# Shared gate and up matmuls at three unit boundaries of an interleaved convolution and FFN kernel

## The chip, the cores and the metric

The kernel runs on one core of one Trainium2 chip. The metric is the device time of one execution in microseconds; less is better. The matrix engine is called TensorE (PE in the profile, its weight loads PEld), the others VectorE (DVE), ScalarE (ACT), GpSimd (POOL) and SyncE (SP), which here only issues DMAs. Matmuls write to PSUM, and VectorE or ScalarE must copy ("evacuate") a result from there before its buffer is free again.

## The reference

Two layers of the same two blocks, on x of 2048 rows and 512 columns (D), in bf16. Block A is a gated long convolution over the rows, block B a SwiGLU feed-forward network with F = 1792:

```python
def _A_ref(q, k, v, shift_k, ssm_k, ssm_D):      # cut to what matters
    k_shift = sum(k_pad[:, t:t + S, :] * shift_k[:, ks - 1 - t] for t in range(4))
    kv = k_shift * v
    y = irfft(rfft(kv_pad) * rfft(kf_pad))[:S]    # causal convolution with ssm_k, by column
    return q * (y + kv * ssm_D)

def _B_ref(x, w_gate, w_up, w_down):
    return (silu(x @ w_gate) * (x @ w_up)) @ w_down

x = A_q
x = x + _A_ref(_layernorm(x), A_k, A_v, A_shift_k, A_ssm_k, A_ssm_D)
x = x + _B_ref(_layernorm(x), B_w_gate, B_w_up, B_w_down)
x = x + _A_ref(_layernorm(x), A_k, A_v, A_shift_k, A_ssm_k, A_ssm_D)
x = x + _B_ref(_layernorm(x), B_w_gate, B_w_up, B_w_down)
```

The convolution's result y depends on k, v and ssm_k alone, so both layers use the same y.

## The kernel before, in words

**Blocks and units.** The rows are cut into four blocks c of 512 rows. A partition p holds four rows (4p to 4p+3) of a block, so a tile of a block is 128 partitions x 4 x 512. A unit (layer, c, h) is one half of a block in one layer: h = 0 holds rows 0 and 2 of each partition, h = 1 rows 1 and 3, 256 rows in all (W). The units follow one another as (0, c, 0), (0, c, 1), (1, c, 0), (1, c, 1) for c = 0 to 3.

**Convolution.** `conv(c)` transforms block c of the kernel and of kv by matmuls with cosine and sine tables (`by_residue`, `direct`), combines spectra on VectorE (`butterfly4`, `product`) and transforms back (`inverse`) to y of that block. Block 0 is done first, in a form of its own (`half`, `direct`, `inverse_half`), since all else waits for it. Blocks 2 and 3 are worked in between the units.

**Prologue.** `prologue(layer, c, h)` normalises a unit's rows, multiplies by y, adds to x, normalises again to z and turns z around into zT, so that the columns of D lie on the partitions: 128 x 4 (contraction tiles) x 256 rows. SP's DMA transposes do the turning (line 893), but for the first unit, where TensorE does (line 920). The statistics of a normalisation are taken by VectorE (`ln_stats`, line 809) or, for chosen units, by ScalarE (`ln_stats_act`): there a Copy with an accumulated sum per row (line 828), a step that scales the sums to negative means (`nm`, line 831), a Square around the mean (line 834), a step that makes the variance (line 838); the power of -1/2 is taken on GpSimd.

**FFN.** `ffn(unit)` goes over the 14 column tiles of F in groups of 4, 4, 4 and 2 (`GROUPS`). For each pair of column tiles TensorE computes gate and up: the weight's 128 x 128 tile is the stationary operand, zT's 256 columns move, four matmuls are added up for a tile, and two tiles fill a PSUM buffer of 512 columns (ring `pf`, line 311 through `mm`). ScalarE evacuates the gate with Silu (line 970) and the up part with a copy (line 974), VectorE multiplies the two of a whole group (line 977), and the down matmuls (line 990, ht stationary, 512 columns of w_down moving) add into two accumulators `pd`, one for each row of the partition. At a unit's end ScalarE copies them (line 1034), VectorE adds them to x (line 1037), and in layer 1 SP stores the rows (line 1045). The last unit, (1, 3, 1), splits its last accumulator by columns, 256 and 256: VectorE finishes one half (line 1008), ScalarE the other (line 1011), and each is stored by its own queue (line 1014).

**What sets the order.** Every step is registered by `plan.add` in program order with its engine, the buffers that it reads and writes and an assumed cost. A table written out by hand, `ORDER`, has one number for each step, its place; `Plan.order` sorts by it, and each engine issues its steps in that order, SP's DMAs too. Buffers of a ring (four `pf`, two `pd`, five `ht`, two `sg`, three `zT`) are handed out along that order. `Plan.issue` emits the steps, and where the plan has a hole on TensorE ahead of 32 us it puts in matmuls of no use (`warm`, line 1267) on a tile of constants, `wz`:

```python
if start < warm_until and start - t > 0.5:
    ...
    n = int((start - max(t, 0.3) - 0.3) / 0.106)
    if n > 0:
        warm(ring, i, n)
```

Waits between engines are worked out from the buffers' regions when the program is built.

Of the kernel before, what the change touches and what calls it, by code (L numbers as in the profile page):

```python
# [18 lines left out]
NB = 4  # L19
# [31 lines left out]
LASTV = True  # L51
ORDER = [
# [58 lines left out]
]  # L111
R = 4

# [125 lines left out]
def kernel(  # L239
# [984 lines left out]
    def run(unit):  # L1224
        ffn(unit)
# [75 lines left out]
```

## Time and profile before

| | |
|---|---|
| median of 3 runs | 344.79 us (344.21 to 345.18) |
| the profiled execution | 344.93 us |
| its span, from the first to the last instruction | 343.2 us |
| TensorE busy | 336.4 us, 2579 matmuls |
| VectorE, ScalarE, GpSimd busy | 283.4, 253.9, 35.3 us |
| DMA | 22.95 MB, 67 GB/s in the mean |
| first gate matmul | 33.6 us |

The profile is of one execution. A row of a group has the line of the kernel, the engine, the operation, what it writes and reads, the shape, how many, the busy time and the mean of one. Matmuls are pipelined: the duration that a record gives is longer than the time from one start to the next, so the time that a stream of them takes is read from the chain of work in order of time, where each piece has its start, its length and its count. "<-" behind a time names what ended the idle time before it. A few matmul records are missing from the trace.

### The profile page before, as it was taken

What the parts mean: (1) busy time and instruction counts of PE and PEld (TensorE: products, weight loads), DVE (VectorE), ACT (ScalarE), POOL (GpSimd) and SP (SyncE); (2) the same over time, 40 slices, a digit from 0 to 9 for tenths busy, and PEclk for the clock granted to TensorE, in tenths of its full rate; (3) what the DMA queues carried; (4) which work ended last, traced back from release to release, by engine and by line L of the source; (5) the groups of instructions that cost most, each with busy time, mean ns of one, the idle gap of its engine ahead of it and who ended that gap; (6) DMA issues with size and microseconds to landing.
All of it is one profiled execution on the core that took longest, in us unless ns stands there. A gap on an engine that the chain in (4) does not pass through costs nothing.

```text
span 343.2 us, 6553 instructions
## 1 busy us (share of the span) xinstructions
PE 336.4 (98%) x2579; PEld 248.6 (72%) x2610; DVE 283.4 (83%) x482; ACT 253.9 (74%) x504; POOL 35.3 (10%) x46
## 2 busy tenths in 40 slices
PE   8999999999999999999999999999999999999996
PEld 7756868768687676858586777768685877777783
DVE  8899999899999999899999999989998433726022
ACT  6999999899997765958789995779475464446261
POOL 4010100203111000103110100201101001000000
PEclk9999999999999999999999999999999999999999
DMA  7999218310116044040101014210101100110101
GB/s 273 336 316 341 52 27 112 77 32 0 34 31 94 14 95 138 2 94 3 32 2 46 2 46 79 76 32 1 32 0 33 35 13 0 39 39 8 24 26 37
DMA packets 42088, 22.95 MB, mean 67 GB/s; under 512 B 33861, under 2 KB 39882, under 8 KB 42058
## 3 DMA queue, kind: packets, MB, share of 16 engines
q1 hardware_dynamic: 41904, 22.47, 26.6%
q8 instruction: 20, 0.33, 0.4%
q14 instruction: 10, 0.08, 0.1%
q10 hardware_dynamic: 154, 0.07, 0.1%
HBM read 12.33 MB, written 2.10 MB: 42 GB/s over the span
## 4 chain that ended last, share of the span: by engine, by line
PE 91%; ACT 4%; DVE 3%; issue 1%
PE pf L311 54%; PE pd L990 28%; PE ps L311 6%; PE ps L458 1%; ACT H L419 1%; PE wm L1267 1%; DVE bnst L809 1%; ACT hs L487 1%; PE pt L477 1%; ACT X L419 0%; ACT n L859 0%; PE pt L366 0%; DVE m L540 0%; DVE t L665 0%; DVE Z L667 0%
## 5 line engine op out<-in xcount | busy, mean ns | idle before, releaser
L311 PE MATMUL pf<-zT,wu_sb 128*128 128x256 bf16 x896 | 110.4, 273 | 0.1
L311 PE MATMUL pf<-zT,wg_sb 128*128 128x256 bf16 x896 | 110.2, 273 | 0.2
L990 PE MATMUL pd<-wd_sb,ht 128*128 128x512 bf16 (+1 forms) x440 | 102.4, 372 | 1.2
L311 PEld LDWEIGHTS <-wu_sb 128*128 128x128 bf16 x896 | 87.7, 98 | 16.4
L311 PEld LDWEIGHTS <-wg_sb 128*128 128x128 bf16 x896 | 87.6, 98 | 16.5 <-issue 0.8
L974 ACT CAST ht<-pf 128x512 bf16<-128x512 f32 x112 | 64.0, 591 | 29.3 <-PE pf L311 29.1
L970 ACT ACTIVATE sg<-pf 128x512 bf16<-128x512 f32 x112 | 65.5, 603 | 17.4 <-PE pf L311 15.1
L990 PEld LDWEIGHTS <-ht 128*128 128x128 bf16 x462 | 45.2, 98 | 42.5
L977 DVE TENSOR_TENSOR ht<-ht,sg 128x1024 bf16<-128x1024 bf16 (+1 forms) x64 | 39.0, 617 | 24.0 <-ACT sg L970 18.7
L814 POOL TENSOR_TENSOR rstd<-ve,nhalf 128x2 f32<-128x2 f32 x24 | 23.0, 958 | 217.8 <-DVE ve L812 207.6
L1034 ACT CAST dn<-pd 128x512 bf16<-128x512 f32 x30 | 17.0, 589 | 21.0 <-PE pd L990 20.9
L809 DVE BATCH_NORM_STATS2 bnst<-xc 128x6 f32<-128x512 bf16 x48 | 31.6, 684 | 0.6
L419 ACT ACTIVATE X<-ps 128x512 bf16<-128x512 f32 x32 | 19.2, 611 | 4.0 <-PE ps L311 3.4
L653 DVE TENSOR_TENSOR t<-X,G 128x2048 bf16<-128x2048 bf16 x18 | 21.9, 1218 | 0.1
L657 DVE TENSOR_TENSOR t<-X,G 128x2048 bf16<-128x2048 bf16 x18 | 21.9, 1216 | 0.0
L1037 DVE TENSOR_TENSOR xc<-xc,dn 128x1024 bf16<-128x1024 bf16 x15 | 10.3, 689 | 13.4 <-ACT dn L1034 13.2
L665 DVE TENSOR_TENSOR t<-t,t 128x2048 bf16<-128x2048 bf16 x12 | 14.7, 1222 | 0.3
L667 DVE TENSOR_TENSOR Z<-Z,t 128x2048 bf16<-128x2048 bf16 x12 | 14.6, 1220 | 0.2
L840 POOL TENSOR_TENSOR rstd<-ve,nhalf 128x2 f32<-128x2 f32 x8 | 8.7, 1088 | 59.2 <-ACT ve L838 59.1
L419 ACT ACTIVATE H<-ps 128x512 bf16<-128x512 f32 x24 | 13.8, 610 | 0.1
L886 DVE TENSOR_TENSOR n<-n,Yk 128x1024 bf16<-128x1024 bf16 x15 | 10.3, 688 | 4.1 <-ACT n L859 3.8
L604 ACT ACTIVATE kc<-kTb,tapF 128x512 bf16<-128x512 bf16 x16 | 12.1, 783 | 0.0
(105 smaller groups left out, 323.3 us busy)
## 6 DMA issues: line engine op xcount, KB each, us to landing
hn<-in_A_ssm_k_dram SPq DMA_DIRECT2D x4, 512.0 KB, 4.1
vt<-in_A_v_dram SPq DMA_DIRECT2D x4, 512.0 KB, 5.9
xc<-in_A_q_dram SPq DMA_DIRECT2D x4, 512.0 KB, 5.3
out_dram<-xc SPq DMA_DIRECT2D x15, 128.0 KB, 1.8
wg_sb<-in_B_w_gate_dram SPq DMA_DIRECT2D x1, 1792.0 KB
wu_sb<-in_B_w_up_dram SPq DMA_DIRECT2D x1, 1792.0 KB, 8.5
wd_sb<-in_B_w_down_dram SPq DMA_DIRECT2D x1, 1280.0 KB, 12.0
kn<-in_A_k_dram SPq DMA_DIRECT2D x1, 512.0 KB, 4.5
```

The costliest lines, as they stand in the source:

```text
L311: nc.tensor.matmul(o, lhsT=lhsT, rhs=rhs, start=(n == 0), stop=(n == len(terms) - 1))
L419: add("ACT", act(D), lambda: nc.scalar.activation(out=view(), in_=ps.t[:], func=ACT.Copy, scale=scale), r=[ps], w=[(buf, keys)], conv=conv)
L653: dve(n * D, lambda t1=t1, part=part: nc.vector.tensor_mul(out=t1.t[:], in0=x.t[:, sl, 0, :], in1=g.t[:, sl, part, :]), [(x, key(slots, (0 ...
L657: dve(n * D, lambda t2=t2, part=part: nc.vector.tensor_mul(out=t2.t[:], in0=x.t[:, sl, 1, :], in1=g.t[:, sl, 1 - part, :]), [(x, key(slots ...
L665: dve(n * D, lambda t1=t1, t2=t2, comb=comb: nc.vector.tensor_tensor(out=t1.t[:], in0=t1.t[:], in1=t2.t[:], op=comb), [t2], [t1], conv=conv)
L809: add("DVE", 0.6, lambda st=st, i=i: nc.vector.bn_stats(out=st.t[:], in_=xs[c].t[:, i, :]), r=[(xs[c], (i,))], w=[st])
L814: add("POOL", pw, lambda: nc.gpsimd.tensor_tensor(out=rstd.t[:], in0=ve.t[:], in1=nhalf.t[:].to_broadcast((P, n)), op=ALU.pow), r=[ve, nha ...
L970: add("ACT", act(D), lambda ps=ps, o=o, sg=sg: nc.scalar.activation(out=sg.t[:, o:o + 2, :], in_=ps.t[:], func=ACT.Silu), r=[ps], w=[(sg, ...
L974: add("ACT", act(D), lambda ps=ps, o=o, ht=ht: nc.scalar.copy(out=ht.t[:, o:o + 2, :], in_=ps.t[:]), r=[ps], w=[(ht, (o // 2,))], due=(uni ...
L977: dve(n * W, lambda sg=sg, ht=ht: nc.vector.tensor_mul(out=ht.t[:], in0=ht.t[:], in1=sg.t[:]), [sg], [ht], due=(unit, k / pairs, 0.0, "h"))
L990: nc.tensor.matmul((pds[o] if not cs.start else pds[HP]).t[:, cs], lhsT=ht.t[:, q, o * P:(o + 1) * P], rhs=wt["d"].t[:, ft, cs], start=(ft ...
L1034: add("ACT", act(D), lambda o=o: nc.scalar.copy(out=dn.t[:, o, :], in_=pds[o].t[:]), r=[pds[o]], w=[(dn, (o,))], due=(unit, 1.0, 3.0, "h"))
```

## The change

**Sharing.** `SHARE` names three units, (1, 0, 1), (0, 2, 0) and (1, 3, 0), whose last two column tiles (12 and 13) are computed for that unit and the next one together. `gate_up(us, fts, k)` is given one or two units. For two, the moving operand takes the 256 columns of both units' zT, 512 in all, so one column tile fills a PSUM buffer; Silu, copy and multiply go over both units' values, and `ht` holds both. The first unit uses its part in its last down matmuls; the next unit begins with the down matmuls of its own part (`left`) and then has the tiles 0 to 11 in three groups of four. So that one access can reach two units' zT, the three slots of the zT ring become slots of one tile, `zall`.

**Means.** In `ln_stats_act` the Copy that sums a row is given the scale -1/D, so its sum is the negative mean, and the step on line 831 is gone, eight times.

**Warming.** The warming matmuls read a constant of ones that the framework sets up, so the memset of `wz` is gone; the number of them is counted to the planned start of the next step where the hole begins between 0 and 8 us, and otherwise 0.3 us short of it.

**Tail.** The last accumulator is split at column 320 (`TAIL`) in place of 256.

**Orders.** `prologue(1, c, 0)` is registered ahead of unit (0, c, 1), and `ORDER` is a new table, of 1556 numbers where there were 1568: nine steps are gone with the memset and the means, and three multiplies are merged into others. A second way to make the variance is in the code but switched off (`VE_D = False`).

```diff
+TAIL = 320
+VE_D = False
+SHARE = {(1, 0, 1): 2, (0, 2, 0): 2, (1, 3, 0): 2}
 ORDER = [
...
-                            n = int((start - max(t, 0.3) - 0.3) / 0.106)
+                            n = int((start - t - (0.0 if 0.0 < t < 8.0 else 0.3)) / 0.106)
...
+        if ring == "zT":
+            def cut(slot):
+                if zall.t is None:
+                    zall.t = zall.make(0)
+                return zall.t[:, slot]
+            return plan.buf(ring, name, cut, parts)
...
+    zall = whole("zT", [P, NZ, KD, HP, P])
...
-                    out=jk.t[:], in_=xs[c].t[:, i, :], func=ACT.Copy, accum_out=sm.t[:, o:o + 1]), r=[(xs[c], (i,))], w=[jk, (sm, (o,))], after=after)
-        nm = new("mv", "nm", [P, n], F32)
-        add("ACT", TINY, lambda: nc.scalar.mul(out=nm.t[:], in_=sm.t[:, 0:n], mul=-1.0 / D), r=[(sm, range(n))], w=[nm])
+                    out=jk.t[:], in_=xs[c].t[:, i, :], func=ACT.Copy, scale=-1.0 / D, accum_out=sm.t[:, o:o + 1]), r=[(xs[c], (i,))], w=[jk, (sm, (o,))], after=after)
+        nm = sm
...
+    def gate_up(us, fts, k):
+        m, n = len(us), len(fts)
+        per = 2 // m
+        sg = new("sg", "sg", [P, n, m, W], parts=n // per)
+        ht = new("ht", "ht", [P, n, m, W], parts=n // per)
+        zs = [zts[u] for u in us]
+
+        def moving(kd):
+            if m == 1:
+                return zs[0].t[:, kd]
+            lo, hi = sorted(z.slot for z in zs)
+            return zall.t[:, lo:hi + 1:hi - lo, kd]
+        for b in range(n // per):
+            sl = slice(b * per, b * per + per)
+            for which in ("g", "u"):
+                ps = new("pf", "pf", [P, D], F32)
+
+                def go(ps=ps, b=b, which=which):
+                    for q in range(per):
+                        ft = fts[b * per + q]
+                        mm(ps.t[:, q * m * W:(q + 1) * m * W],
+                           [(wt[which].t[:, kd, ft * P:(ft + 1) * P], moving(kd)) for kd in range(KD)])
...
+        dve(n * m * W, lambda: nc.vector.tensor_mul(out=ht.t[:], in0=ht.t[:], in1=sg.t[:]), [sg], [ht], due=(us[0], (k + n) / NF, 0.0, "h"))
+        return ht
+
+    def down(unit, pds, ht, fts, us, k, first, end, own):
...
+            halves = (slice(0, TAIL), slice(TAIL, D))
...
+                    at = sorted(zts[u].slot for u in us).index(zts[unit].slot)
+                    for cs in css:
+                        for q, ft in enumerate(fts):
+                            nc.tensor.matmul((pds[o] if not cs.start else pds[HP]).t[:, cs], lhsT=ht.t[:, q, at, o * P:(o + 1) * P],
+                                             rhs=wt["d"].t[:, ft, cs], start=(first and q == 0 and not own(o, cs)),
+                                             stop=(end and q == len(fts) - 1))
...
+        left, nxt = shared.pop(unit, []), UNITS[UNITS.index(unit) + 1] if unit != LAST_UNIT else None
+        rest = [ft for ft in range(NF) if all(ft not in fts for _, fts, _ in left)]
+        cut = len(rest) - SHARE.get(unit, 0)
+        groups = left + [(None, rest[a:min(a + 4, cut)], (unit,)) for a in range(0, cut, 4)] \
+            + [(None, rest[a:a + 2], (unit, nxt)) for a in range(cut, len(rest), 2)]
...
-    wz = whole("wz", [P, P])
-    add("DVE", 0.07, lambda: nc.vector.memset(wz.t[:], 0.5), w=[wz], due=-80)
+    ones = nc.const_aps.tensor(1.0, (P, P), BF16)
...
         run((0, c, 0))
+        prologue(1, c, 0)
         run((0, c, 1))
-        prologue(1, c, 0)
         prologue(1, c, 1)
...
-            nc.tensor.matmul(t[:], lhsT=wz.t[:], rhs=wz.t[:], start=True, stop=True)
+            nc.tensor.matmul(t[:], lhsT=ones, rhs=ones, start=True, stop=True)
```

More of the change, by code (lines that the diff above doesn't have):

```diff
@@ L51 @@
 LASTV = True
+TAIL = 320
+VE_D = False
+SHARE = {(1, 0, 1): 2, (0, 2, 0): 2, (1, 3, 0): 2}
 ORDER = [
[58 rows of a table removed]
[57 rows of a table added]
 ]
 R = 4
+NZ = 3
 NS = 8
@@ L231, in issue @@
                 if b.t is None:
-                    b.t = b.make(place.get(b, 0))
+                    b.slot = place.get(b, 0)
+                    b.t = b.make(b.slot)
                 if b in place:
@@ L835, in ln_stats_act @@
                 out=jk.t[:], in_=xs[c].t[:, i, :], func=ACT.Square, bias=nm.t[:, o:o + 1], accum_out=sm.t[:, n + o:n + o + 1]),
-                r=[(xs[c], (i,)), nm], w=[jk, (sm, (n + o,))])
+                r=[(xs[c], (i,)), (nm, (o,))], w=[jk, (sm, (n + o,))])
         ve, rstd = new("ve", "ve", [P, n], F32), new("rs", "rstd", [P, n], F32)
-        add("ACT", TINY, lambda: nc.scalar.activation(out=ve.t[:], in_=sm.t[:, n:2 * n], func=ACT.Identity, scale=1.0 / D, bias=eps.t[:]),
-            r=[(sm, range(n, 2 * n)), eps], w=[ve])
+        if VE_D:
+            add("DVE", 0.08, lambda: nc.vector.tensor_scalar(out=ve.t[:], in0=sm.t[:, n:2 * n], scalar1=1.0 / D, scalar2=LN_EPS,
+                                                             op0=ALU.mult, op1=ALU.add), r=[(sm, range(n, 2 * n))], w=[ve])
+        else:
+            add("ACT", TINY, lambda: nc.scalar.activation(out=ve.t[:], in_=sm.t[:, n:2 * n], func=ACT.Identity, scale=1.0 / D, bias=eps.t[:]),
+                r=[(sm, range(n, 2 * n)), eps], w=[ve])
         add("POOL", PWA, lambda: nc.gpsimd.tensor_tensor(out=rstd.t[:], in0=ve.t[:], in1=nhalf.t[:].to_broadcast((P, n)),
@@ L930 @@
     LAST_UNIT = (1, NB - 1, HP - 1)
+    UNITS = [(layer, c, h) for c in range(NB) for layer in (0, 1) for h in range(HP)]
+    shared = {}
+    def gate_up(us, fts, k):
[18 more added lines that the diff above has]
+                           [(wt[which].t[:, kd, ft * P:(ft + 1) * P], moving(kd)) for kd in range(KD)])
+                at = (k + b * per) / NF
+                add("PE", pe(per * KD, m * W), go, r=[*zs, wt[which]], w=[ps], due=(us[0], at + (which == "u") / 21, 0.0, None))
+                if which == "g":
+                    add("ACT", act(D), lambda ps=ps, sl=sl: nc.scalar.activation(out=sg.t[:, sl], in_=ps.t[:], func=ACT.Silu),
+                        r=[ps], w=[(sg, (b,))], due=(us[0], at, 1.0, "a"))
+                else:
+                    add("ACT", act(D), lambda ps=ps, sl=sl: nc.scalar.copy(out=ht.t[:, sl], in_=ps.t[:]),
+                        r=[ps], w=[(ht, (b,))], due=(us[0], at, 1.5, "a"))
+        dve(n * m * W, lambda: nc.vector.tensor_mul(out=ht.t[:], in0=ht.t[:], in1=sg.t[:]), [sg], [ht], due=(us[0], (k + n) / NF, 0.0, "h"))
+        return ht
@@ new lines, in down, with go @@
+    def down(unit, pds, ht, fts, us, k, first, end, own):
+        for o in range(HP):
+            last = unit == LAST_UNIT and end and o == HP - 1
+            split = unit == LAST_UNIT and o == HP - 1
+            halves = (slice(0, TAIL), slice(TAIL, D))
+            cols = [[cs] for cs in halves] if last else [halves] if split else [[slice(0, D)]]
+            for css in cols:
+                def go(o=o, css=css):
+                    at = sorted(zts[u].slot for u in us).index(zts[unit].slot)
[4 more added lines that the diff above has]
+                                             stop=(end and q == len(fts) - 1))
+                n = len(fts)
+                add("PE", pe(n) if not last else pe(n, css[0].stop - css[0].start), go,
+                    r=[ht, (wt["d"], sorted({int(ft >= GROUPS[0]) for ft in fts}))],
+                    w=[pds[o]] if not split else [pds[o], pds[HP]] if not last else [pds[HP if css[0].start else o]],
+                    due=(unit, k / NF, 2.0, None))
@@ L944, in ffn @@
                 i = row(h, o)
-                halves = (slice(0, D // 2), slice(D // 2, D)) if unit == LAST_UNIT and o == HP - 1 else (slice(0, D),)
+                halves = (slice(0, TAIL), slice(TAIL, D)) if unit == LAST_UNIT and o == HP - 1 else (slice(0, D),)
                 halves = [cs for cs in halves if own(o, cs)]
@@ new lines, in ffn @@
+        left, nxt = shared.pop(unit, []), UNITS[UNITS.index(unit) + 1] if unit != LAST_UNIT else None
[3 more added lines that the diff above has]
+            + [(None, rest[a:a + 2], (unit, nxt)) for a in range(cut, len(rest), 2)]
+        k = 0
+        for n, (ht, fts, us) in enumerate(groups):
+            if ht is None:
+                ht = gate_up(us, fts, k)
+                if len(us) > 1:
+                    shared.setdefault(nxt, []).append((ht, fts, us))
+            k += len(fts)
+            down(unit, pds, ht, fts, us, k, n == 0, n == len(groups) - 1, own)
@@ L1004, in ffn @@
                 due=(unit, 1.0, 20.0, None))
-            for half_, (eng, cs) in enumerate((("DVE", slice(0, D // 2)), ("ACT", slice(D // 2, D)))):
+            for half_, (eng, cs) in enumerate((("DVE", slice(0, TAIL)), ("ACT", slice(TAIL, D)))):
                 copy = nc.scalar.copy if eng == "ACT" else nc.vector.tensor_copy
                 if LASTV and not half_:
-                    add(eng, 0.35, lambda cs=cs: nc.vector.tensor_add(out=x.t[:, i, cs], in0=x.t[:, i, cs], in1=pds[o].t[:, cs]),
+                    add(eng, 0.42, lambda cs=cs: nc.vector.tensor_add(out=x.t[:, i, cs], in0=x.t[:, i, cs], in1=pds[o].t[:, cs]),
                         r=[pds[o], (x, (i,))], w=[(x, (R + half_,))], due=(unit, 1.0, 3.0, "h"))
                 else:
-                    add(eng, 0.35, lambda cs=cs, copy=copy, half_=half_: copy(out=x.t[:, i, cs], in_=pds[HP if half_ else o].t[:, cs]),
+                    add(eng, 0.3, lambda cs=cs, copy=copy, half_=half_: copy(out=x.t[:, i, cs], in_=pds[HP if half_ else o].t[:, cs]),
                         r=[pds[HP if half_ else o]], w=[(x, (R + half_,))], due=(unit, 1.0, 3.0, "h"))
```

42 lines of the change are left out of this document (1 added, 41 removed), and 115 rows, old and new, of the table ORDER.

## The prediction

> **What bounds the kernel now.** I read the page's head and its chain first, then busy time by stage, then TensorE's waits, then the timelines of the first 34 us and the last 4 us.
>
> ```profile
> span 343.2 us, 6553 instructions
> ...
> PE 336.4 (98%) x2579; PEld 248.6 (72%) x2610; DVE 283.4 (83%) x482; ACT 253.9 (74%) x504; POOL 35.3 (10%) x46
> ...
> PE 91%; ACT 4%; DVE 3%; issue 1%
> ```
>
> TensorE is busy for 98% of the span and carries 91% of the chain that ended last. A share of busy time can hide holes, so the waits must say whether they are there (engine and line, who released it, total, times, longest):
>
> ```profile
> PE wm L1267 <- DVE wz L1050: 1.0, 1, 1.0
> PE ps L311 <- ACT H L419: 0.4, 1, 0.4
> PE ps L311 <- DVE vt L515: 0.4, 1, 0.4
> ```
>
> These three are all the waits that the trace puts down to TensorE, and the timeline has all three in the first 32 us:
>
> ```profile
> 1.04 2.53 PE L1267 MATMUL wm<-wz 128*128 128x128 bf16 x22 [1.04 <-DVE wz L1050]
> ...
> 24.51 0.38 PE L311 MATMUL ps<-hs,fwd 128*128 128x512 bf16 x1 [0.40 <-ACT H L419]
> ...
> 31.25 0.39 PE L311 MATMUL ps<-vt,fwd 128*128 128x512 bf16 x1 [0.35 <-DVE vt L515]
> ```
>
> From the first gate matmul at 33.6 us to the last down matmul near 340 us TensorE waits for nobody. By stage (stretch, its length, then busy time of PE, PEld, DVE, ACT, POOL, the clock, the DMA share and GB/s):
>
> ```profile
> 0.00:10.00 10.00, 8.85 (x74) 7.14 (x76) 7.74 (x28) 6.67 (x13) 3.64 (x14) 1.00 0.81 292
> 10.00:20.00 10.00, 9.95 (x100) 6.76 (x100) 9.48 (x17) 8.89 (x22) 1.04 (x1) 1.00 1.12 306
> 20.00:30.00 10.00, 9.50 (x84) 6.05 (x85) 9.93 (x22) 10.00 (x20) 0.00 (x0) 1.00 1.04 355
> 30.00:40.00 10.00, 9.60 (x93) 7.75 (x92) 9.64 (x18) 9.94 (x25) 1.65 (x2) 1.00 0.82 178
> ...
> 180.00:220.00 40.00, 39.79 (x307) 30.11 (x309) 39.04 (x52) 32.88 (x64) 2.19 (x2) 1.00 0.24 53
> ...
> 260.00:300.00 40.00, 39.84 (x298) 29.23 (x299) 20.38 (x48) 20.08 (x37) 4.07 (x5) 1.00 0.10 24
> ```
>
> So there are two regimes. After 33.6 us a change pays only by taking matmul time from TensorE or by ending the tail sooner; relief for VectorE and ScalarE is worth nothing there. Before 33.6 us three engines are near full together, and there alone are holes to close.
>
> **The change, part by part.** The sum is made against the profiled execution, 344.93 us: 343.2 us of span and 1.73 us around it. The median of the runs is 344.79 us, 0.14 us lower.
>
> The wide matmuls first. The rows of the chain in order of time (start, length, what, how many) give the price of a column:
>
> ```profile
> 4.49 1.86 PE pt L477 x16
> 6.35 0.85 PE pt L366 x8
> ...
> 9.03 0.45 PE pt L366 x8
> ...
> 165.89 2.59 PE pd L990 x12
> ...
> 266.73 13.10 PE pf L311 x120
> ```
>
> Gate and up run at 13.10/120 = 109.2 ns for 256 columns, the down matmuls at 2.59/12 = 215.8 ns for 512. At one boundary two column tiles, two weights, four contraction tiles and two units make 32 narrow matmuls; they become 16 wide ones. Over three boundaries 96 x 109.2 ns = 10.48 us becomes 48 x 215.8 ns = 10.36 us: **-0.12 us**. The moving operand of a wide one comes in two pieces from two slots, which no row shows. Its bounds are no saving at all (it costs two narrow ones) and the -0.12 us; I take the latter, since each piece is a whole row of 256 columns, as in the narrow ones.
>
> [...]
>
> What else the sharing does costs nothing on the path. ScalarE evacuates as many 512-column tiles as before. VectorE multiplies one tile of 1024 where it had two of 512, three times, and eight row statistics lose a small ScalarE step each:
>
> ```profile
> 317.26 0.60 ACT L970 ACTIVATE sg<-pf 128x512 bf16<-128x512 f32 x1 [1.15 <-PE pf L311]
> ```
>
> ```profile
> 315.84 0.68 DVE L977 TENSOR_TENSOR ht<-ht,sg 128x1024 bf16<-128x1024 bf16 x1
> ...
> 317.89 0.43 DVE L977 TENSOR_TENSOR ht<-ht,sg 128x512 bf16<-128x512 bf16 x1 [1.04 <-ACT sg L970]
> ```
>
> ```profile
> L831 ACT ACTIVATE nm<-sm x8: 202/209/269, 13.3 to 236.2; 128x2 f32<-128x2 f32 x8
> ```
>
> That is 3 x (2 x 0.43 - 0.68) = 0.5 us of VectorE and 8 x 0.21 = 1.7 us of ScalarE, seven of the eight behind 33.6 us, where TensorE's matmuls cover them. Without that cover they would be worth up to those 2.2 us. Making the z tiles slots of one tile adds no instruction; the prologue that is moved in the program moves only numbers in the order table. No DMA is added; SP has the same transposes and stores and POOL the same steps, in another order. The two down matmuls of a shared group open the next unit's accumulators, and must wait, as its first ones did, until ScalarE has copied out the unit before; TensorE has gate and up steps to put in between.
>
> The tail. Its timeline, and the copy of 512 columns beside it:
>
> ```profile
> 338.69 0.69 DVE L998 TENSOR_TENSOR xc<-xc,pd 128x512 bf16<-128x512 bf16 x1 [2.09 <-PE pd L990]
> ...
> 339.78 0.42 DVE L1008 TENSOR_TENSOR xc<-xc,pd 128x256 bf16<-128x256 bf16 x1 [0.40 <-PE pd L990]
> 340.00 0.37 ACT L1011 CAST xc<-pd 128x256 bf16<-128x256 f32 x1 [4.12 <-PE pd L990]
> ...
> 340.40 0.38 ACTq L1014 DMA_DIRECT2D out_dram<-xc  x1
> ```
>
> ScalarE's copy starts when the last matmul is done and issues the last store. From 0.60 us for 512 columns and 0.37 us for 256, 64 columns fewer are 0.06 us. VectorE's 320 columns are 0.07 us longer (0.69 - 0.42 = 0.27 us per 256), but begin four matmuls of 192 columns ahead of the end (4 x 0.082 = 0.33 us) where it was two of 256 (0.22 us), so they end no later. **-0.05 us**. The last group now holds four tiles in place of two, and 14 matmuls of other groups, 3.0 us, stand between its last gate or up matmul and its own down ones; evacuation and multiply, 0.60 + 0.68 us and their hand-overs, fit under that.
>
> The start. The warming matmuls need no memset any more and run longer before the transposes; they are filler, and at the same clock that costs nothing, because the first transposes wait for a load that is untouched. What remains is the order. Read against the list of steps, the new table puts the same 83 TensorE steps ahead of the first gate or up matmul and the same VectorE work, less one memset, ahead of the first two z. Thus only waits can go. VectorE's:
>
> ```profile
> 7.24 0.69 DVE L374 COPY kTb<-pt 128x512 bf16<-128x512 bf16 x1 [0.58 <-PE pt L366]
> ...
> 9.52 0.69 DVE L374 COPY kTb<-pt 128x512 bf16<-128x512 bf16 x1 [0.62 <-PE pt L366]
> ...
> 15.45 0.69 DVE L447 TENSOR_TENSOR G<-ev 128x1024 bf16<-128x1024 bf16 x1 [0.37 <-ACT ev L419]
> ...
> 31.45 0.73 DVE L864 TENSOR_SCALAR z<-xc,mv,rstd 128x512 bf16<-128x512 bf16 x2
> ```
>
> The first stays, since the k transposes come as late as before. The second goes, for both k transposes that VectorE copies now come early, but VectorE then meets TensorE, which is busy for 9.95 of 10 us from 10 to 20 us and hands over little sooner. The third can go whole: the two evacuations that the last spectrum needs now stand together, ahead of the second Square, and one step of means is gone from that queue. Bounds: all three, -1.57 us; or a new wait like TensorE's of 0.40 us above, +0.4 us. I take **-0.3 us**, near the 0.37 us row. What is late next is VectorE itself, 9.93 of 10 us busy from 20 to 30 us.
>
> Sum: -0.12 - 0.05 - 0.3 = -0.47 us, 344.46 us in such a profile, **344.3 us** as a median.
>
> **The rivals.** *The clock opens sooner (faster).* The rows above have 8 transposes of 128 columns in 0.85 us up to 7.2 us, and 8 in 0.45 us from 9.03 us on: TensorE begins at half pace, though the clock column says 1.00. The 24 transposes up to 7.2 us, 1.86 + 0.85 us, would take 1.35 us at the later pace. If warming that starts at 0.8 us and leaves no hole opens it before 4.5 us, up to 1.36 us go: 344.3 - 1.1 = 343.2 us with some of it lost to loads. Against it: the opening came 6 us after the first matmul, and nothing shows that 0.24 us more of filler moves it. [...] Its time also stands for the three start waits all going.
>
> *The wide matmuls are much cheaper than their columns.* At most they could cost what a narrow one does, 48 x 0.107 us = 5.1 us: 339.2 us. [...]
>
> *The second unit's z is late at a boundary (slower).* A shared matmul needs both units' z. At the third boundary (1, 3, 0) the new table leaves behind the first shared matmul 4 shared steps (3.45 us), 12 steps of eight narrow matmuls (10.48 us) and down matmuls worth 32 x 0.2158 = 6.91 us: 20.84 us ahead of the end of the matmuls, which ScalarE's copy at 340.00 us follows at once, so it starts at 319.1 us on the old clock. The old transposes for that z:
>
> ```profile
> 316.00 2.50 SPq L893 DMA_TRANSPOSE zT<-z  x2
> ```
>
> ```profile
> DMA to landing us min/median/max: 2.3/2.4/4.2
> ```
>
> The second is issued near 317.3 us and lands at 319.7 us, 0.6 us too late. Against it: the new table takes two ScalarE evacuations (1.2 us) from ahead of that prologue's normalisation and a multiply (0.6 us) from between its statistics. If that gain fails and the landing is the slowest, 4.2 us, the wait is 0.6 + 1.8 = 2.4 us: 346.7 us. It decides the sign from a landing of 320.6 us on.
>
> *The new order starves TensorE elsewhere* because VectorE, 39.04 of 40 us busy from 180 to 220 us, is late for a z: two waits of that 2.4 us less the gain, 348.6 us. Counted in VectorE's work, the z steps and their statistics stand at most some 2.5 us behind their old places and mostly ahead of them, which speaks against it.
>
> **How the numbers follow.** About 0.3%, 1.03 us, is what a measurement of this kernel can tell from no change. Forecast 0.45, range 343.5 to 345.1 us by its bounds (start -1.1 to +0.4); early clock or closed waits 0.32; cheap wide matmuls 0.01; late z 0.12; starved elsewhere 0.10. Faster is 0.32 + 0.01 = 0.33, same 0.45, slower 0.12 + 0.10 = 0.22. The range for 8 in 10 reaches from 342.8 us (the fast rival with the sum's bound) to 346.5 us, most of the late z.
>
> **What would show it.** Right: 48 matmuls of 512 columns on z at about 216 ns; still no wait on TensorE behind the first gate matmul; that matmul 0 to 0.7 us sooner; the ScalarE copy of 192 columns near 0.31 us. Wrong: transposes of 56 ns before 7 us (fast rival), a TensorE wait for a DMA at a boundary, wide matmuls apart from 216 ns, or waits between 40 and 320 us.

## The result and the profile after

The changed kernel takes 343.7 us in the median (343.22 to 344.02, 8 runs), the kernel before on the same chip 344.6 us (344.19 to 345.18, 8 runs): ratio 0.9976, 95% interval 0.9967 to 0.9985. That is 0.24% less, inside the 0.3% that count as no change. The forecast was 344.3 us; the profiled execution took 343.72 us.

The page's head of the changed kernel, its chain, and all waits put down to TensorE:

```profile
span 341.9 us, 6474 instructions
...
PE 337.6 (99%) x2566; PEld 243.4 (71%) x2566; DVE 282.5 (83%) x478; ACT 252.5 (74%) x496; POOL 37.0 (11%) x46
...
PE 93%; ACT 3%; DVE 1%; DMA 1%; issue 0%; POOL 0%; POOLq 0%; ACTq 0%
```

```profile
PE wm L1307 <- PEq L1325: 0.8, 1, 0.8
PE pf L323 <- DMA zT<-z: 0.3, 1, 0.3
```

The span is 1.22 us shorter (343.15 to 341.93). The wait of 1.0 us for `wz` has become one of 0.8 us for TensorE's own sequencer (PEq), and the two of 0.4 us at 24.51 and 31.25 us are gone. New is one that the sum had put at nothing: TensorE waits for a z transpose in the body, which the prediction had named as a sign of being wrong. By stage (columns as before) the start is fuller, and 260 to 300 us is less full:

```profile
0.00:10.00 10.00, 9.19 (x93) 7.59 (x94) 8.37 (x29) 6.64 (x14) 3.60 (x14) 1.00 0.79 282
...
20.00:30.00 10.00, 9.94 (x86) 5.99 (x84) 9.62 (x22) 9.93 (x20) 0.20 (x1) 1.00 1.05 353
...
260.00:300.00 40.00, 39.68 (x295) 28.66 (x294) 20.92 (x46) 19.25 (x35) 2.77 (x4) 1.00 0.12 28
```

TensorE's timeline of the start (start, length), then VectorE's waits, the first z and the first gate or up matmul:

```profile
0.76 2.83 PE L1307 MATMUL wm<-const-bfloat16-1.0 128*128 128x128 bf16 x25 [0.76 <-PEq L1325]
...
3.74 1.03 PE L1307 MATMUL wm<-const-bfloat16-1.0 128*128 128x128 bf16 x8
4.83 1.32 PE L489 MATMUL pt<-ident,hn 128*128 128x128 bf16 x16
5.99 0.83 PE L378 MATMUL pt<-ident,kn 128*128 128x128 bf16 x12
...
10.79 0.69 DVE L536 TENSOR_TENSOR vt<-ps,vt 128x512 bf16<-128x512 f32 x1 [0.96 <-PE ps L323]
...
14.79 0.69 DVE L457 TENSOR_TENSOR G<-ev 128x1024 bf16<-128x1024 bf16 x1 [0.26 <-ACT ev L431]
...
30.64 0.73 DVE L879 TENSOR_SCALAR z<-xc,mv,rstd 128x512 bf16<-128x512 bf16 x2
...
32.58 1.69 PE L323 MATMUL pf<-zT,wu_sb 128*128 128x256 bf16 x14
```

The first gate or up matmul comes 1.00 us sooner (33.58 to 32.58). Sixteen transposes take 1.32 us where they took 1.86, so TensorE came to full pace while they ran; but they begin at 4.83 us where they began at 4.49. The tail:

```profile
338.67 0.49 DVE L1049 TENSOR_TENSOR xc<-xc,pd 128x320 bf16<-128x320 bf16 x1 [0.73 <-PE pd L994]
339.00 0.32 ACT L1052 CAST xc<-pd 128x192 bf16<-128x192 f32 x1 [4.56 <-PE pd L994]
...
339.35 0.38 ACTq L1055 DMA_DIRECT2D out_dram<-xc  x1
```

So the difference of the spans has three parts: the start -1.00 us; the body, from the first gate or up matmul to ScalarE's last copy, 306.42 us in both (340.00 - 33.58 and 339.00 - 32.58), so 0; the tail, from that copy to the end of the span, 3.15 to 2.93, -0.22 us. The runs had to say why the start gave three times what was forecast, and why the body gave nothing, not even the 0.12 us of the wide matmuls.

### The profile page after: what moved, and what is told of

The parts are those of the page before. It is cut to its first block, busy times and chain, and to the rows that moved or that the text cites. A ratio compares the mean times of both kernels' runs of the same rounds, so it can differ in the third digit from the quotient of the medians.

```text
span 341.9 us, 6474 instructions
## 1 busy us (share of the span) xinstructions
PE 337.6 (99%) x2566; PEld 243.4 (71%) x2566; DVE 282.5 (83%) x478; ACT 252.5 (74%) x496; POOL 37.0 (11%) x46
## 4 chain that ended last, share of the span: by engine, by line
PE 93%; ACT 3%; DVE 1%; DMA 1%; issue 0%; POOL 0%; POOLq 0%; ACTq 0%
PE pf L323 56%; PE pd L994 27%; PE ps L323 6%; PE ps L470 2%; DMA zT<-z 1%; ACT H L431 1%; PE wm L1307 1%; PE pt L489 1%; ACT Yk L729 1%; ACT ks L526 0%; ACT n L874 0%; DVE bnst L821 0%; ACT Yk L703 0%; PE pt L378 0%; DVE xc L902 0%
## 5 line engine op out<-in xcount | busy, mean ns | idle before, releaser
L323 PE MATMUL pf<-zT,wu_sb 128*128 128x256 bf16 (+1 forms) x872 | 110.0, 275 | 0.4 <-DMA zT<-z 0.3
L323 PE MATMUL pf<-zT,wg_sb 128*128 128x256 bf16 (+1 forms) x872 | 110.3, 276 | 0.0
L994 PE MATMUL pd<-wd_sb,ht 128*128 128x512 bf16 (+1 forms) x462 | 106.2, 373 | 0.0
L323 PEld LDWEIGHTS <-wu_sb 128*128 128x128 bf16 x872 | 85.2, 98 | 19.5 <-DMA zT<-z 0.8
L323 PEld LDWEIGHTS <-wg_sb 128*128 128x128 bf16 x872 | 85.3, 98 | 17.3
L977 ACT CAST ht<-pf 128x512 bf16<-128x512 f32 x112 | 64.8, 590 | 23.7 <-PE pf L323 23.4
L974 ACT ACTIVATE sg<-pf 128x512 bf16<-128x512 f32 x112 | 66.3, 603 | 20.7 <-PE pf L323 17.3
L826 POOL TENSOR_TENSOR rstd<-ve,nhalf 128x2 f32<-128x2 f32 x24 | 25.1, 1046 | 193.1 <-DVE ve L824 193.1
L855 POOL TENSOR_TENSOR rstd<-ve,nhalf 128x2 f32<-128x2 f32 x8 | 8.4, 1048 | 79.3 <-ACT ve L853 79.3
L323 PE MATMUL ps<-hs,fwd 128*128 128x512 bf16 x40 | 12.7, 379 | 0.1
```

The costliest lines, as they stand in the source:

```text
L323: nc.tensor.matmul(o, lhsT=lhsT, rhs=rhs, start=(n == 0), stop=(n == len(terms) - 1))
L826: add("POOL", pw, lambda: nc.gpsimd.tensor_tensor(out=rstd.t[:], in0=ve.t[:], in1=nhalf.t[:].to_broadcast((P, n)), op=ALU.pow), r=[ve, nha ...
L974: add("ACT", act(D), lambda ps=ps, sl=sl: nc.scalar.activation(out=sg.t[:, sl], in_=ps.t[:], func=ACT.Silu), r=[ps], w=[(sg, (b,))], due=( ...
L977: add("ACT", act(D), lambda ps=ps, sl=sl: nc.scalar.copy(out=ht.t[:, sl], in_=ps.t[:]), r=[ps], w=[(ht, (b,))], due=(us[0], at, 1.5, "a"))
L994: nc.tensor.matmul((pds[o] if not cs.start else pds[HP]).t[:, cs], lhsT=ht.t[:, q, at, o * P:(o + 1) * P], rhs=wt["d"].t[:, ft, cs], start ...
```

## The experiments

Two numbers of each profile carry the argument. The *opening* is where TensorE comes to full pace: the first three 128-column matmuls in a row under 60 ns apart, or the first of 512 columns that takes 216 ns, from the starts in the trace. The trace also has a record of the granted clock. It begins, with full speed, at 7.28 us in the kernel before and at 5.43 us in the changed one, and in all profiles but e11's, which has none, 0.01 to 0.25 us ahead of the opening that the starts give. Ahead of that record there is none, and the clock column of the views prints 1.00 there, though 128-column matmuls take 107 ns. The *body* is worked out as above. A row's ratio is to the kernel before on the same chip; the rows come from several chips, so medians of different rows are compared with care.

| kernel | warming | opening | first gate or up | body | median, ratio to before [95%] |
|---|---|---|---|---|---|
| before | old | 7.36 | 33.58 | 306.42 | 344.6 |
| after | new | 5.49 | 32.58 | 306.42 | 343.7, 0.9976 [0.9967, 0.9985] |
| e1 | new | 5.62 | 32.96 | 306.66 | 344.47, 0.9994 [0.9969, 1.0019] |
| e2 | old | 7.36 | 33.28 | 305.93 | 343.68, 0.9969 [0.9950, 0.9989] |
| e3 | old | 7.10 | 34.29 | 306.23 | 344.99, 1.0017 [1.0002, 1.0032] |
| e4 | old | 7.09 | 33.53 | 306.18 | 344.38, 1.0005 [0.9989, 1.0021] |
| e5 | old | 4.61 | 32.54 | 306.19 | 343.98, 0.9986 [0.9975, 0.9997] |
| e6 | new | 3.98 | 32.59 | 306.05 | 343.4, 0.9975 [0.9961, 0.9989] |
| e7 | none | 7.87 | 33.57 | 305.93 | 344.64, 1.0002 [0.9977, 1.0027] |
| e8 | new | 4.83 | 32.30 | 307.26 | 344.81, 1.0013 [1.0003, 1.0023] |
| e9 | new, 3 fewer | 5.65 | 32.56 | 306.60 | 344.0, 0.9995 [0.9983, 1.0007] |
| e10 | new | 5.72 | 32.94 | 306.43 | 344.1, 0.9989 [0.9976, 1.0002] |
| e11 | old | 5.51 | 32.44 | 305.92 | 343.3, 0.9972 [0.9957, 0.9987] |
| e12 | new, 3 fewer | 6.79 | 33.05 | 305.94 | 343.09, 0.9963 [0.9950, 0.9975] |

**Warming alone (e1)**, in the kernel before:

```diff
-                            n = int((start - max(t, 0.3) - 0.3) / 0.106)
+                            n = int((start - t - (0.0 if 0.0 < t < 8.0 else 0.3)) / 0.106)
...
-            nc.tensor.matmul(t[:], lhsT=wz.t[:], rhs=wz.t[:], start=True, stop=True)
+            nc.tensor.matmul(t[:], lhsT=ones, rhs=ones, start=True, stop=True)
```

> The kernel before with the new warming alone (a constant of ones in place of the memset tile, and the holes ahead of 8 us filled to the end). Theory A, the clock: the start is sooner because TensorE reaches its full pace near 5.5 us in place of 7.2 us; then nearly all of the 1.0 us shows here, first gate matmul at 32.6 to 32.9 us, 343.8 us. Theory B, the order: the 1.0 us comes from the new order of the start; then first gate at 33.6 us and 344.6 us, whatever the pace does.

The opening was at 5.62 us, the first gate or up matmul 0.62 us sooner, the body 0.24 us longer, and the time the same. Neither theory has it whole: the start went with the opening, as theory A says, but 0.38 us of the 1.00 us are missing, and the time didn't follow.

**The change with the old warming (e2, and once more as e11)**, the same edit backwards, with the memset of `wz`:

> The changed kernel with the old warming (memset tile and old count). Theory A: full pace comes near 7.2 us again, first gate at 33.3 to 33.6 us, 344.5 us. Theory B: first gate stays at 32.6 us, 343.7 us.

> The changed kernel with the old warming (memset, old count), against the changed kernel of the same call. If the sooner full pace of the clock carries to the end, this is 0.5 to 0.7 us slower in the median. If the sooner start is absorbed before the end, or by executions in which the clock opens early under either warming, the two medians are within 0.2 us. Profile: full pace from 7.1 to 7.4 us, first gate matmul 33.2 to 33.3 us.

At an equal opening of 7.36 us the first gate or up matmul is 0.30 us sooner than in the kernel before (33.58 to 33.28): this is the order's part. A second pair with nearly equal openings, e1 and the changed kernel (5.62 and 5.49 us), gives 0.38 us, of which the opening's 0.13 us at half pace is some 0.07. The time was no longer than with the new warming, and beside the changed kernel on one chip (e10) it was shorter: 343.3 to 344.1 us, 0.9977 (0.9967 to 0.9993 by resampling the runs). The bodies of e2 and e11 are 0.49 us shorter than the changed kernel's; e10 and e12 say why. e11 also took away what I had begun to believe, that the new warming is what opens the clock sooner. TensorE's first matmuls of these two profiles of one and the same kernel:

```profile
1.04 2.53 PE L1309 MATMUL wm<-wz 128*128 128x128 bf16 x22 [1.04 <-DVE wz L1092]
...
4.49 1.87 PE L490 MATMUL pt<-ident,hn 128*128 128x128 bf16 x16
```

```profile
4.49 1.51 PE L490 MATMUL pt<-ident,hn 128*128 128x128 bf16 x16
```

The first is e2's, the second e11's. The same filler, the same start, and the opening at 7.36 us in the one and 5.51 us in the other.

**The order of the start alone (e3)**: the kernel before, with its 234 steps ahead of the first gate or up matmul in the new order and the rest in its own.

> The kernel before with the steps ahead of the first gate or up matmul in the changed kernel's order (234 steps) and the rest in its own; old warming, old tail, no sharing. Theory A: first gate at 33.4 to 33.6 us, 344.6 us. Theory B: first gate at 32.6 to 32.9 us, 343.8 us. Both hold in part if it comes between, near 344.2 us.

A miss. At the seam of the two orders TensorE met a wait of its own, which neither kernel has:

```profile
34.07 0.38 PE L311 MATMUL ps<-vt,fwd 128*128 128x512 bf16 x1 [0.69 <-ACT X L419]
```

So this run can't say what the new order of the start is worth; that is read from e2.

**The tail alone (e4)**, the split at 320 in the kernel before:

```diff
-                halves = (slice(0, D // 2), slice(D // 2, D))
+                halves = (slice(0, 320), slice(320, D))
```

> The kernel before with its last accumulator split at column 320 in place of 256, nothing else. By the prediction's sum: ScalarE's last copy 0.32 us in place of 0.37 us, 344.6 - 0.05 = 344.55 us. Rival: the smaller last store also lands sooner, and the 3.15 us from that copy's start to the end of the span become 2.9 us, as in the changed kernel's profile: 344.4 us.

```profile
339.71 0.32 ACT L1011 CAST xc<-pd 128x192 bf16<-128x192 f32 x1 [4.12 <-PE pd L990]
```

The copy took 0.32 us, but from its start to the end of the span it was 3.41 us, where it is 3.15 in the kernel before and 2.93 in the one after. With the old order that last stretch scatters: 2.98 us in e3 and e5 and 3.15 to 3.17 in the kernel before and e1, all four with the old split, and 3.41 here. In the nine profiles with the new order it is 2.93 to 2.96 us, 0.02 to 0.05 below the lowest of the old split. So the profiles allow the 0.05 us, and the rest of the tail's 0.22 us is the late end of the one profile before.

**The means alone (e5)**: in the kernel before, the scale in the Copy and no `nm` steps; each Square now waits for its own row's mean alone, as in the changed kernel.

```diff
-                    out=jk.t[:], in_=xs[c].t[:, i, :], func=ACT.Copy, accum_out=sm.t[:, o:o + 1]), ...
-        nm = new("mv", "nm", [P, n], F32)
-        add("ACT", TINY, lambda: nc.scalar.mul(out=nm.t[:], in_=sm.t[:, 0:n], mul=-1.0 / D), ...
+                    out=jk.t[:], in_=xs[c].t[:, i, :], func=ACT.Copy, scale=-1.0 / D, accum_out=sm.t[:, o:o + 1]), ...
+        nm = sm
```

> The kernel before with one part of the change: the Copy that sums a row carries the scale -1/D, and the eight steps on ScalarE that made the means of the sums are gone, the order otherwise as before. If the 1.7 us of ScalarE lie under the matmuls, as I forecast, nothing is seen but at most 0.2 us sooner at the start, where one of the eight stands: 344.3 to 344.6 us, ratio 0.9990 to 1.0005. If ScalarE's time mattered in the body, the span would be up to 1.7 us shorter, ratio 0.995. The eight rows of 0.2 us are missing from the profile in any case.

The body, 306.19 us, is that of e4, which has the eight steps (306.18): 1.7 us of ScalarE are worth nothing there. The median fell by 0.56 us, more than I expected, with an interval that reaches to 0.9997. Of VectorE's three waits at the start two stand, 0.56 and 0.37 us; the 0.62 us is gone, behind the earliest opening under the old warming. Ahead of that opening TensorE's start is that of the kernel before:

```profile
4.49 1.07 PE L479 MATMUL pt<-ident,hn 128*128 128x128 bf16 x16
```

So how much of the 0.56 us belongs to the edit stays open.

**Narrow in place of wide (e6)**: the changed kernel, each shared matmul as two of 256 columns, one per unit.

```diff
-                        mm(ps.t[:, q * m * W:(q + 1) * m * W],
-                           [(wt[which].t[:, kd, ft * P:(ft + 1) * P], moving(kd)) for kd in range(KD)])
+                        for j, z in enumerate(sorted(zs, key=lambda z: z.slot)):
+                            mm(ps.t[:, (q * m + j) * W:(q * m + j + 1) * W],
+                               [(wt[which].t[:, kd, ft * P:(ft + 1) * P], z.t[:, kd]) for kd in range(KD)])
```

> The changed kernel with each shared matmul of 512 columns issued as two of 256, one for each unit, into the same buffers and in the same order. By the prediction's first term: 96 narrow matmuls of 109.2 ns in place of 48 of 215.8 ns, +0.12 us, 343.8 us. If wide matmuls were much cheaper than their columns, up to +5 us; if the two-piece moving operand cost something, less than 343.7 us.

Its body is 306.05 us; those of e2, e7, e11 and e12, the same order with wide matmuls, are 305.92 to 305.94. The difference is 0.12 us, the forecast price, and too little to be seen in the medians. That this kernel has no hole near 265 us was the first hint that the hole was not the order's.

**No warming (e7)**: the changed kernel without its filler.

> The changed kernel with no warming matmuls at all. Theory A: the full pace then comes later still, some 5 to 6 us behind the first transposes at 4.4 us, near 10 us; the matmuls between 5.5 and 10 us take twice as long and the first gate comes 1 to 2 us later, 34 us; with theory C, 0.5 us of that is hidden at 265 us: 344.3 to 345.2 us. Rival: the pace has nothing to do with the warming; 343.7 us or, since the transposes then begin 0.3 us sooner, less.

The opening came last of all, at 7.87 us, but not near 10, and the first gate or up matmul at 33.57 us, 0.29 us behind e2's with the old warming. The time was that of the kernel before (344.64 us).

**The hole near 265 us: another queue (e8, e9).** My second theory was that the z transpose is late because SP's queue hands out two of them one behind the other. In e8 one of that unit's two goes out on ScalarE's queue; e9 has this edit and fills the second warming hole only to 0.3 us short.

```diff
+                qn, q = ("ACT", nc.scalar) if (layer, c, h) == (0, 3, 0) and o == 0 else ("SP", nc.sync)
-                add("SP", 1.25, lambda z=z, o=o: nc.sync.dma_start_transpose(
+                add(qn, 1.25, lambda z=z, o=o, q=q: q.dma_start_transpose(
```

> The changed kernel with one of the two transposes of unit (0, 3, 0)'s z issued from ScalarE's queue, ahead of its evacuations, in place of SP's second place. Theory C: the sooner start of the changed kernel (first gate at 32.6 us against 33.3 us with the old warming) is mostly given back at 265 us, where TensorE waits 0.48 us for that z; then the wait goes, and the time is 0.4 to 0.5 us less than the changed kernel's, 343.25 us or 0.9961 of before. Rival: VectorE, 98% busy up to 260 us, holds the next units' z as late too, and the wait turns up again at (0, 3, 1) near 278 us; then 343.7 us.

> As the run with the transpose on ScalarE's queue, and the second hole of the start filled only up to 0.3 us ahead of its planned end, as the old count did (ones as constant, sooner first matmul kept). In the new warming's profiles the first transposes begin at 4.83 us, in the old one's at 4.49 us: the longer filler holds them back. If the full pace comes by the sooner first matmul, it stays near 5.6 us and the start gains 0.3 us more: 343.0 us. If it comes by the hole's filling, the pace turns near 7.2 us, first gate at 33.2 us, 343.7 us.

Neither was better than the changed kernel: 344.81 us (1.0013 [1.0003, 1.0023]) and 344.0 us (0.9995 [0.9983, 1.0007]). ScalarE's and SP's timeline and TensorE's wait in e8:

```profile
259.63 1.19 SPq L910 DMA_TRANSPOSE zT<-z  x1
262.21 1.97 ACTq L910 DMA_TRANSPOSE zT<-z  x1
264.22 0.60 ACT L976 ACTIVATE sg<-pf 128x512 bf16<-128x512 f32 x1 [4.61 <-issue]
```

```profile
PE pd L996 <- DVE ht L981: 1.2, 1, 1.2
```

The second transpose was issued only when the first had landed, at 262.21 us behind a landing at 262.04 and 2.58 us behind the first one's issue, and ScalarE stood behind it for 4.61 us, so the next Silu, its multiply and the down matmuls were late. The hole on TensorE is 1.33 us in place of 0.48, and the median 1.1 us above the changed kernel's in the first comparison: what the body loses is not given back. e9 has a hole of 0.66 us from the same cause. Its opening stayed early, 5.65 us, but its transposes waited for their load until 4.63 us, and the 343.0 us that I had hoped for didn't come.

**The hole itself (e10, e12).** e10 is the changed kernel again, without an edit.

> The changed kernel itself once more, beside the same with the old warming and beside the new means alone, all on one chip, because the differences in question are 0.3 to 0.7 us. If the slow landing of one z transpose (4.0 us in place of 2.3 to 2.5) was a single event of one execution, this profile has no wait of TensorE for zT behind the first gate matmul, the full pace again from before 6 us, a first gate matmul at 32.3 to 32.7 us and a span of 341.4 to 341.7 us. If it belongs to the kernel, the wait of some 0.5 us near 265 us is there again and the span is 341.9 us. Median 343.2 to 343.7 us against 344.5 us of before.

The hole is there again, and the body is 306.43 us. It belongs to the kernel. The median, 344.1 us, is above what I expected: in this profile TensorE also stood 0.23 us for the load of `kn`, until 6.34 us, so that its first gate or up matmul came 0.36 us later than in the profile after, though the opening was only 0.23 us later. In the profile after, the two transposes and the matmul that waits:

```profile
259.91 2.50 SPq L908 DMA_TRANSPOSE zT<-z  x2
...
265.20 1.05 PE L323 MATMUL pf<-zT,wu_sb 128*128 128x256 bf16 x8 [0.32 <-DMA zT<-z]
```

The second is issued near 261.15 us and lands at 265.15, some 4 us later, where the median of z transposes is 2.5. The DMA view of the stretch 263.0 to 264.2 us says what else moved:

```profile
q1 hardware_dynamic: 84, 0.01, 6.3%
q8 instruction: 1, 0.02, 5.4%
```

One packet of instructions, 16 KB, runs on one DMA engine from 263.09 to 264.12 us, just as the transpose's last packets go out. Of the transpose's 16 completion marks in the trace 15 lie from 263.48 to 263.63 us and one at 265.15; of e10's, 15 from 263.84 to 263.99 and one at 265.52, with such a packet from 263.5 us on. In e11 the packet comes at 264.5 us and all 16 marks lie within 0.16 us. There are 20 such packets in a profile, some 17 us apart. That they are TensorE's is read from e6 and e12, which change TensorE's instructions alone: in e6, which has more of them by then, packets come at 257.0 and 274.2 us and none between, and in e12, which has six fewer, one comes at 265.4 us in place of 263.09. In the profile after TensorE begins 249 matmuls and weight loads from one of the 20 packets to the next in the mean.

All 14 profiles together bear this out. Of the 303 z transposes whose landing the traces tell, 16 landed 4.0 to 4.3 us behind their issue, and each of the 16 had such a packet begin while it was under way, 15 of them 1.8 to 2.0 us behind the issue; no transpose with a packet there landed sooner. The 257 without a packet beside them have a median of 2.4 us and at most 3.8. The 4.2 us that the prediction quoted from the kernel before is one of the 16. It was issued at 240.81 us, and the DMA view of the stretch 240.7 to 245.1 us has the packet beside it:

```profile
q8 instruction: 1, 0.02, 1.6%
zT<-z SPq DMA_TRANSPOSE x2, 3.8
```

The changed kernel has two more, at 85.76 and 190.31 us, which TensorE doesn't feel; it feels the one whose z it needs at once. e1 has a hole of 0.27 us at 245 us behind a transpose that landed after 3.9 us, with a packet 1.0 us behind its issue: its filler moved a packet too, and that is its longer body.

So fewer warming matmuls should move the packet off the transpose. e12 is the changed kernel with three of 35 less:

```diff
-                            n = int((start - t - (0.0 if 0.0 < t < 8.0 else 0.3)) / 0.106)
+                            n = int((start - t - (0.0 if 0.0 < t < 3.0 else 0.3)) / 0.106)
```

> The changed kernel with the second warming hole filled only to 0.3 us short of the first transposes, as in the kernel before: three warming matmuls fewer, nothing else. Theory of the instruction transfer: in the two profiles of the changed kernel a transfer of 16 KB of instructions lies on one of the 16 DMA engines right behind the z transpose issued near 261 us, 15 of 16 completions come in time and the last 1.7 us later; TensorE's instructions are what it carries, so fewer of them ahead shift it, to 264.5 to 266 us, where it meets nothing TensorE waits for. Then no wait on TensorE for zT, no hole near 265 us, and the holes behind the first gate matmul are 0.03 us in place of 0.53; the first hn transposes start at 4.49 to 4.63 us in place of 4.83; the first gate matmul at 32.4 to 32.6 us if the pace opens near 5.6 us; span 341.2 to 341.5 us, median 343.2 to 343.5 us. Rival, that the wait comes from the order of SP's queue, which the last runs with the same order and another warming speak against: the wait of 0.3 to 0.5 us is there again, span 341.7 us or more.

Its chain, the start of its transposes, the place of the hole, and what the DMA view has for the stretch 260.2 to 264.2 us:

```profile
PE 96%; ACT 3%; issue 0%; ACTq 0%
```

```profile
4.50 1.86 PE L489 MATMUL pt<-ident,hn 128*128 128x128 bf16 x16
...
260.40 2.50 SPq L908 DMA_TRANSPOSE zT<-z  x2
...
265.20 1.04 PE L323 MATMUL pf<-zT,wu_sb 128*128 128x256 bf16 x8
```

```profile
q1 hardware_dynamic: 1088, 0.26, 33.2%
issues: line engine op xcount, KB each, median us to landing
out_dram<-xc SPq DMA_DIRECT2D x1, 128.0 KB
zT<-z SPq DMA_TRANSPOSE x2, 2.5
```

The packet came at 265.4 us, 232.4 us behind the first gate or up matmul, where it was 230.5 and 230.6 in the two profiles of the changed kernel. Both transposes landed in time though they were issued 0.5 us later than in the changed kernel, the hole is gone, and the body is 305.94 us. The transposes of the start began at 4.50 us. Only the opening was late in this profile, 6.79 us, so its span of 341.9 us missed the 341.2 to 341.5 us that I had set. The median, 343.09 us, is the lowest of all kernels run: 0.9963 of the kernel before. Its interval meets the changed kernel's, so the profile shows that the hole is gone, and the medians alone don't show what that is worth.

## Why the prediction was right, and where its steps failed

The kernel came out 0.9 us faster in the first comparison and 0.44 us in the second (e10), where 0.47 us were forecast, and both are within 0.3%. The three terms of the sum hold. That the total came out so near is in part luck: the profiled execution gained an early opening and two closed holes that I had not counted, and lost again two things that I had put at nothing.

- **What bounds the kernel** held in the main. TensorE is busy for 99% of the span, and of the 1.7 us that ScalarE lost in means nothing is seen in the body (e5). Nor is it of the 0.5 us of VectorE: e6 has the merged multiplies, and its body of 306.05 us is that of the old order without its holes (below).
- **Wide matmuls, -0.12 us**, right. Four of them stand in the chain at 107.14 us with 0.86 us (the row is below): 215 ns each, so the rival that had them much cheaper than their columns is not seen. The moving operand in two pieces costs nothing beside the 215.8 ns of a down matmul, and e6 has the 0.12 us in the body.
- **The start's order, -0.3 us**, right in size: -0.30 us at an equal opening (before and e2), and some -0.31 in the second pair (e1 and after). The row I took it from was only part of it. VectorE's 0.37 us became 0.26 and not zero, the 0.62 went, a new one of 0.96 came; and TensorE's own two waits of 0.40 and 0.35 us, which I quoted and then left out of the sum, are gone.
- **The warming, "at the same clock that costs nothing, because the first transposes wait for a load that is untouched"**: this step failed. In the profile after the load's last completion mark is at 4.24 us, and with the filler the transposes began at 4.83. e12, with three matmuls less, began them at 4.50: 0.33 us. Less filler can't gain much more, for the load lands as late as 4.5 to 4.6 us in other profiles (e7 and e9 wait for it until 4.57 and 4.63).
- **"From the first gate matmul at 33.6 us to the last down matmul near 340 us TensorE waits for nobody", and "No DMA is added"**: the first failed too, for both kernels. No DMA was added, but 20 packets of instructions come by DMA as well, by e6 and e12 TensorE's, and with three matmuls of filler less one came at 265.4 us in place of 263.1. The kernel before has two holes that its waits view doesn't list, one of 0.16 us near 64 us and one of 0.21 near 132. Ahead of the second, twenty down matmuls from 127.89 us are done at 132.21, at 215.8 ns each; the matmuls behind it need a z whose transpose was issued at 128.48 us and landed only at 132.29 (rows below). The new order closes both, 0.37 us that I had not counted. The bodies of the kernel before, e1, e4 and e5 without such holes (0.37, 0.60, 0.17 and 0.15 us) are all 306.0 to 306.1 us, as e6's is; with wide matmuls it is 305.93, the 0.12 us of the sum. In the changed kernel the instruction packet then put 0.48 us on top, so that both bodies measure 306.42 us is chance. I had costed the filler's clock and nothing of its instructions.
- **The tail, -0.05 us**: the copy took 0.32 us, as forecast; the rest of the 0.22 us in the spans is scatter behind it (e3 to e5).
- **Late z at a shared boundary**: no. At the third one the transposes are issued at 313.20 us in place of 316.00, and no wait is there. The price I gave this rival, a landing of some 4 us, was paid at another unit, and by a cause that the prediction didn't have.
- **The early clock**: in the profile its sign was there (transposes at 56 ns before 7 us), and it is 0.7 of the 1.00 us at the start. But it isn't shown to be the change's: with the old warming the opening lay at 4.61, 5.51, 7.09, 7.10, 7.36 and 7.36 us, with the new one at 3.98, 5.49, 5.62, 5.72 and 6.79, with e8 and e9 at 4.83 and 5.65. That the new warming shifts the odds isn't excluded by so few; in time no gain is seen (e1, and e10 beside e11). What sets the opening no run shows: e2 and e11, one kernel, have it 1.85 us apart.

Two sums of the prediction don't come out. Two waits of 2.4 us on top of the forecast are 349.1 us, where it has 348.6; the gain was taken off twice. And its bound for the start was all three waits, -1.57 us, while its range goes by -1.1. Neither bears on the result.

The row of the chain of the changed kernel, in order of time, on which the wide matmuls rest:

```profile
107.14 0.86 PE pf L323 x4
```

The rows of TensorE's timeline in the kernel before, on both sides of its hole near 132 us:

```profile
127.89 4.48 PE L990 MATMUL pd<-wd_sb,ht 128*128 128x512 bf16 x20
132.43 1.80 PE L311 MATMUL pf<-zT,wg_sb 128*128 128x256 bf16 x15
```

What stays open: why the packet moves by some 2 us for six instructions, where 5132 of them in 342 us would make it 0.4; whether the hole stands in every execution (two profiles of two have it); and the share of the means in e5's median.

## What to carry to other kernels

Before you explain a gain at the start from one profile, look where TensorE comes to full pace: with the old warming it moved by 2.75 us among six profiles, by 1.85 between two of one kernel, and the first gate or up matmul of that kernel with it by 0.84 us. Compare profiles by stretches that begin behind it. Filler had two prices here that its own row doesn't show: it ran past the landing it waits for (the transposes began at 4.83 us, and at 4.50 with three matmuls less), and its instructions shifted what is fetched later (the packet at 263.1 and 265.4 us). When one transfer is late by 1.5 us without a cause on its queue, look for an instruction packet beside it; here three matmuls less moved the packet, and moving the transfer to another queue made things worse (a hole of 1.33 us in place of 0.48).

## What the runs showed of the hardware

With a 16 KB transfer of instructions on one of the 16 DMA engines beside it, the last completion of a z transpose came 1.5 us behind the other 15 (265.15 and 263.63 us in the profile after), and TensorE lost 0.48 us, some 260 us behind the six instructions without which (e12) the transfer came later and the hole was gone; in 14 profiles all 16 z transposes that took 4.0 us or more had such a packet beside them. In e8 the transpose on ScalarE's queue was not issued before SP's had landed (262.21 and 262.04 us), and ScalarE stood for 4.61 us. The clock column reads 1.00 from 2 to 7 us in every profile, also where 128-column matmuls take 107 ns; the trace's record of the clock, which e11's profile lacks, begins in the others only at the opening (3.7 to 7.8 us).
